# One stage more in the attention pipeline of a fused attention and mixer kernel

## The chip, the cores and the metric

The kernel runs on one core of one Trainium2 chip. The metric is device time in microseconds (us), the median of three runs. The core has five engines, each with its own queue that runs strictly in order: PE multiplies matrices (its weight loads are listed as PEld), DVE works on vectors, ACT applies functions and copies, POOL does some vector work, and SP issues most of the transfers. The engines wait for each other through semaphores.

## The reference

Three parts follow each other, on a batch of 4, a sequence of 576 and a width of 512 (8 heads of 64):

```
scores = q @ k.T / 8                       # per batch and head
scores = where(0 <= i - j < 64, scores, -1e9)
attn   = exp(scores - max(scores)); attn /= sum(attn) + 1e-9
x      = heads joined (attn @ v)           # (4, 576, 512)

mixed  = real(fft(fft(x, axis=1), axis=2))
u      = x + mixed;  un = layernorm(u)
x2     = u + relu(un @ w_ch1) @ w_ch2      # 512 -> 2048 -> 512

h      = relu(x2.T @ w_tok1) @ w_tok2      # over the tokens
u2     = x2 + h.T
out    = u2 + relu(u2 @ w_ch1') @ w_ch2'   # 512 -> 1536 -> 512
```

## The kernel before

The window of 64 keys makes attention small. It is cut into 36 units: per batch nine, of which eight hold two blocks of 64 queries for four heads each, and the ninth, the middle unit, holds the last 64 queries of all eight heads. A unit runs through seven small functions:

- `a_s` (L403): on PE, one matmul that writes the mask (L407) and sixteen in 64 x 64 tiles that add the scores (L414), into a PSUM tile `s4`. There are two such tiles, from the pool `pg`.
- `a_mx` (L421): DVE takes the row maxima (L423, tile `mx`), ACT scales them (L425, `nb`).
- `a_ex` (L428): ACT takes four exponentials from `s4` to `pb` (L433). They are the last to read `s4`.
- `a_pt` (L435): PE transposes the four pieces (L440, `pt`). `a_cp` (L442): ACT copies them back to `pb` (L443).
- `a_pv` (L445): PE multiplies with the values (L453, `o`). `a_nx` (L456): DVE divides by the sums (L460, L462, and L465, or two L470 for a middle unit) into `x`.

The loop in `front_body` (L1056) is the pipeline: in its step k it issues pieces of units k, k-1 and k-2. Into each step it also puts work of other kinds, in this order after the attention pieces:

- up to two pieces of the Fourier transform of a finished batch (`chunk`, L1071). PE runs eight matmuls in most (L531), then ACT writes the rounded half of the result and DVE the rest (`split`, L126, so L128 on ACT and L131 on DVE, tile `zt` or `zx`). In the second transform ACT copies one result (L568) and DVE reads it (L581, L582). Of the nine steps after a finished batch eight have such pieces.
- "side" work of DVE, cut by a budget in `left`: folding `x` (`fold`, tiles `pmt`, `eo`, then a split to `xh` or `xs`), splits of constants (`cs`, `dd`), statistics for the layer norm, and the conversion of the first weights (L163 to L185).

The whole front is recorded under a manual schedule, so an engine's queue holds exactly the order in which the Python code issues its work. The rest of the kernel, from about 205 us on, is a long run of matmuls (L694, L712, L729, L773), whose order a scheduler sets.

The names k, k+1 below count units; a step is one turn of the loop at L1056.

Of the kernel before, what the change touches and what calls it, by code (L numbers as in the profile page):

```python
# [29 lines left out]
def kernel(  # L30
# [351 lines left out]
    NU = len(units)  # L382
# [20 lines left out]
    def a_s(i):  # L403
        b, t, par = units[i]
        s4 = pg("s4").rearrange("p (h j) -> p h j", h=4)
        at[i, "s"] = s4
        nc.tensor.matmul(s4, lhsT=idb, rhs=cap[:, CAPS[t]:CAPS[t] + 1, :].to_broadcast([128, 4, 128]), start=True, stop=False)  # L407
        for c in range(4):
            for bl in range(2):
                if par is not None:  # L410
                    r, q0, k0 = par, 128 * (t % 2) + 64 * bl, KEY0[t][bl]
                else:
                    r, q0, k0 = bl, 0, 640
                nc.tensor.matmul(  # L414
                    s4[64 * bl:64 * bl + 64, c, :],
                    lhsT=q_t[b, t // 2][64 * r:64 * r + 64, c, q0:q0 + 64],
                    rhs=kT[b][64 * r:64 * r + 64, c, k0:k0 + 128],
                    start=False, stop=c == 3,
                )

    def a_mx(i):  # L421
        mx = sm([128, 4], F32, name="mx")
        nc.vector.tensor_reduce(out=mx, in_=at[i, "s"], axis=AX.X, op=ALU.max)  # L423
        nb = sm([128, 4], F32, name="nb")
        nc.scalar.mul(nb, mx, -scale)  # L425
        at[i, "nb"] = nb
# [18 lines left out]
    def a_pv(i):  # L445
        b, t, par = units[i]
        pb = at.pop((i, "pb"))
        o = pa("o")[:, 0:4 * (D + 1)].rearrange("p (h d) -> p h d", h=4)
        at[i, "o"] = o
        for c in range(4):  # L450
            for bl in range(2):
                rhs = v_t[b, t][:, bl, 2 * c + par, :] if par is not None else v_t[b, t][:, 0, 2 * c + bl, :]
                mm = nc.tensor.matmul(o[64 * bl:64 * bl + 64, c, :], lhsT=pb[:, 1, c, 64 * bl:64 * bl + 64], rhs=rhs)  # L453
        last_pv[0] = mm.ins

    def a_nx(i):  # L456
        b, t, par = units[i]
        o = at.pop((i, "o"))
        rs = sm([128, 4, 1], F32, name="rs")
        nc.vector.tensor_scalar_add(rs, o[:, :, D:D + 1], 1e-9)  # L460
        ri = sm([128, 4, 1], F32, name="ri")
        nc.vector.reciprocal(out=ri, in_=rs)  # L462
        x = x_tile(b, t).rearrange("p (c r d) -> p c r d", c=4, r=2)
        if par is not None:
            nc.vector.tensor_tensor(out=x[:, :, par, :], in0=o[:, :, 0:D], in1=ri.to_broadcast([128, 4, D]), op=ALU.mult)  # L465
        else:
            h0 = 64 * (b % 2)
            for r in range(2):
                a = slice(64 * r, 64 * r + 64)
                nc.vector.tensor_tensor(  # L470
                    out=x[h0:h0 + 64, :, r, :], in0=o[a, :, 0:D], in1=ri[a].to_broadcast([64, 4, D]), op=ALU.mult
                )
# [460 lines left out]
    if True:  # L933
# [91 lines left out]
        def front_body():  # L1025
            load_const()
            load_k(0, (0, 192))
            load_q(0, 0)
            load_k(0, (192, 576))
            load_v(0, 0)  # L1030
            load_k(0, (576, KW))
            load_v(0, 1)
            load_q(0, 1)
            load_q(0, 2)
            for s in range(2, 5):
                load_v(0, s)
            later = [load_cs(0), load_cs(1)]
            side = []
            ffts = []
            cur = []  # L1040
            evs = []
            side0 = []
            pcount = qcount = 0
            left = 0.0

            def chunk():
                while cur or ffts:
                    if not cur:
                        cur.append(fft(ffts.pop(0)))
                    e = next(cur[0], None)  # L1050
                    if e is not None:
                        return e
                    cur.pop()
                return None

            for k in range(NU + 3):  # L1056
                if k < NU:
                    a_s(k)
                if 0 <= k - 2 < NU:
                    a_pv(k - 2)  # L1060
                if 0 <= k - 1 < NU:
                    a_pt(k - 1)
                    a_cp(k - 1)
                if k < NU:
                    a_mx(k)
                if 0 <= k - 2 < NU:
                    a_nx(k - 2)
                if k < NU:
                    a_ex(k)
                left = min(left, 0.0) + CFG["dve"] - (1.5 if k < NU else 0.7)  # L1070
                for _ in range(2):  # L1071
                    e = chunk() if k >= 2 else None
                    if e:
                        left -= 0.25
                        e()
                if 0 <= k - 2 < NU:
                    b, t, par = units[k - 2]
                    if par == 1 and t in (1, 3):
                        side.append(fold(b, t // 2))
                    if t == 4:  # L1080
                        side.append(fold_m(b))
                while side and left > 0.0:
                    t = next(side[0], None)
                    if t is None:
                        side.pop(0)
                    else:
                        left -= t
                for (b, kt) in list(fst):
                    if kt == 2 and b not in fdone:
                        fdone.add(b)  # L1090
                        ffts.append(b)
                if k in (3, 5):
                    later.pop(0)()
                    left -= 1.1
                    if k == 3:
                        later.append(load_dd())
                if k == 7:
                    later.pop(0)()
                put_stores()
                if k < NU:  # L1100
                    b, j = divmod(k, 9)
                    if j == 1 and b + 1 < B:
                        load_k(b + 1, (0, KW))
                    if j == 3 and b + 1 < B:
                        load_q(b + 1, 0)
                        load_v(b + 1, 0)
                    if j == 5 and b + 1 < B:
                        load_v(b + 1, 1)
                    if j == 7 and b + 1 < B:
                        load_v(b + 1, 2)  # L1110
                        load_q(b + 1, 1)
                    if j == 0 and 0 < b:
                        load_v(b, 3)
                    if j == 1 and 0 < b:
                        load_v(b, 4)
                        load_q(b, 2)
                if k == 20:
                    side0.append(prep(0, u_d, 0, True, res[0, 0], ts=x_of(0)))
                if k == 30:
                    pre1[0] = prep(0, u_d, 1, True, res[1, 0], ts=x_of(1))  # L1120
                while side0 and left > 0.0 and (pcount < 7 or k >= 28):
                    t = next(side0[0], None)
                    pcount += 1
                    if t is None:
                        side0.pop(0)
                    else:
                        left -= t
                    if pcount > 7:
                        break
                while k >= 30 and left > 0.0 and qcount < 7:  # L1130
                    left -= next(pre1[0])
                    qcount += 1
                while k >= 8 and left > 0.0 and njob[0] < 2 * KA:
                    conv(1)
                    left -= 1.0
            while side0:
                if next(side0[0], None) is None:
                    side0.pop(0)
            n = 0
            tailing[0] = 1  # L1140
            while True:
                if n % 4 == 0:
                    next(gph)
                e = chunk()
                if e is None:
                    break
                e()
                if n % 2:
                    conv(1)
                elif n >= 4:  # L1150
                    next(pre1[0], None)
                put_stores()
                n += 1
                tailing[0] = n + 1
            tailing[0] = 0
            while not phase2[0]:
                next(gph)
# [70 lines left out]
        k = CFG["wb0"]  # L1228
# [155 lines left out]
```

## Time and profile before

| | |
|---|---|
| median of three runs | 986.06 us (985.76 to 986.57) |
| the profiled execution | 985.86 us, of which the span of the trace is 984.1 |
| busy share of the span: PE, DVE, ACT, POOL | 96%, 62%, 36%, 12% |
| matmuls | 6413 |

The busy shares are means over stages with different limits. The page's 40 slices show two of them: in the first five slices or so (some 150 us) PE's row changes between 8 and 9 and DVE's is at 7 or above in most, with a dip of PE and of its clock after that, and in the last three quarters PE stands at 9 in nearly every slice. The front is what the change touches; the rest starts when the front has handed over.

### The profile page before, as it was taken

What the parts mean: (1) busy time and instruction counts of PE and PEld (TensorE: products, weight loads), DVE (VectorE), ACT (ScalarE), POOL (GpSimd) and SP (SyncE); (2) the same over time, 40 slices, a digit from 0 to 9 for tenths busy, and PEclk for the clock granted to TensorE, in tenths of its full rate; (3) what the DMA queues carried; (4) which work ended last, traced back from release to release, by engine and by line L of the source; (5) the groups of instructions that cost most, each with busy time, mean ns of one, the idle gap of its engine ahead of it and who ended that gap; (6) DMA issues with size and microseconds to landing.
All of it is one profiled execution on the core that took longest, in us unless ns stands there. A gap on an engine that the chain in (4) does not pass through costs nothing.

```text
span 984.1 us, 16233 instructions
## 1 busy us (share of the span) xinstructions
PE 941.0 (96%) x6413; PEld 833.3 (85%) x6413; DVE 613.1 (62%) x1343; ACT 354.5 (36%) x761; POOL 120.8 (12%) x128
## 2 busy tenths in 40 slices
PE   8898988699999999999999999998999999999997
PEld 5676766587887899999999988876999999999997
DVE  3877777799999266676675324455775445445544
ACT  4655554333333213222232212323543333333332
POOL 0003031242222001112111000011310000000000
PEclk9888979799999999999999999999999999999999
DMA  9843220234443062454554216375411011101000
GB/s 329 295 132 135 102 66 23 91 113 133 125 142 105 5 189 73 146 171 155 174 174 131 71 40 206 108 232 167 128 45 44 1 44 44 44 1 44 23 22 22
DMA packets 58192, 105.61 MB, mean 107 GB/s; under 512 B 5250, under 2 KB 25796, under 8 KB 57732
## 3 DMA queue, kind: packets, MB, share of 16 engines
q1 hardware_dynamic: 57428, 104.25, 32.6%
q8 instruction: 50, 0.82, 0.4%
q10 hardware_dynamic: 688, 0.33, 0.1%
q14 instruction: 26, 0.21, 0.1%
HBM read 79.78 MB, written 24.77 MB: 106 GB/s over the span
## 4 chain that ended last, share of the span: by engine, by line
PE 63%; DVE 14%; DMA 3%; ACT 2%; issue 2%; POOL 0%; SPq 0%; DVEq 0%; ACTq 0%; POOLq 0%
PE zg L694 15%; PE acc L712 15%; PE zg L729 15%; PE acc L773 11%; PE acc L760 3%; PE zt L890 2%; DVE wm L180 2%; DVE we L166 2%; PE tpa L685 1%; PE zt L915 1%; DVE w2s L185 1%; DMA x2r<-x_d 1%; DVE w1s L185 1%; DVE hh L702 1%; DVE rw L179 1%
## 5 line engine op out<-in xcount | busy, mean ns | idle before, releaser
L694 PE MATMUL zg<-aT,w1s 128*128 128x384 f32 x1152 | 224.9, 344 | 3.9 <-DVE hh L702 2.9
L694 PEld LDWEIGHTS zg<-aT,w1s 128*128 128x128 f32 x1152 | 204.1, 191 | 20.1 <-DVE hh L702 12.8
L712 PE MATMUL acc<-w2s,hh 128*128 128x512 f32 x864 | 218.1, 394 | 0.0
L712 PEld LDWEIGHTS acc<-w2s,hh 128*128 128x128 f32 x864 | 160.8, 188 | 29.5
L729 PE MATMUL zg<-aT,wb 128*128 128x256 f32 x1296 | 165.5, 282 | 0.8 <-ACT wb L128 0.8
L729 PEld LDWEIGHTS zg<-aT,wb 128*128 128x128 f32 x1296 | 158.7, 189 | 1.9 <-ACT wb L128 1.0
L182 POOL TENSOR_TENSOR wm<-wm,we 128x512 f32<-128x512 f32 (+2 forms) x64 | 70.7, 1104 | 346.2 <-DVE wm L180 308.4
L702 DVE SCALAR_TENSOR_TENSOR hh<-zg,hh 128x384 fp32r<-128x384 f32 x96 | 53.2, 554 | 88.0 <-ACT hh L701 87.9
L701 ACT ACTIVATE hh<-zg 128x384 fp32r<-128x384 f32 x96 | 47.0, 490 | 168.8 <-PE zg L694 168.5
L773 PE MATMUL acc<-wb,hb 128*128 128x256 f32 x540 | 71.7, 281 | 0.0
L163 ACT ACTIVATE wm<-rw 128x512 f32<-128x512 uint32 (+2 forms) x66 | 41.9, 634 | 80.6 <-DVE w2s L185 38.9
L736 ACT ACTIVATE h<-zg 128x512 f32<-128x512 f32 x54 | 32.3, 599 | 97.1 <-PE zg L729 90.6
L773 PEld LDWEIGHTS acc<-wb,hb 128*128 128x128 f32 x540 | 67.2, 189 | 0.0
L747 DVE TENSOR_TENSOR s4h<-h 128x128 f32<-128x128 f32 x90 | 23.1, 298 | 58.8 <-ACT h L736 58.6
L773 PE MATMUL acc<-wb,ha 128*128 128x256 f32 x405 | 56.3, 281 | 0.0
L773 PEld LDWEIGHTS acc<-wb,ha 128*128 128x128 f32 x405 | 51.7, 189 | 0.2
L131 DVE TENSOR_TENSOR hb<-s4h,hb 128x512 fp32r<-128x512 f32 x45 | 31.4, 698 | 27.8 <-ACT hb L128 27.8
L180 DVE SCALAR_TENSOR_TENSOR wm<-rw,wm 128x512 f32<-128x512 int32 (+2 forms) x66 | 43.4, 658 | 5.2
L166 DVE SCALAR_TENSOR_TENSOR we<-rw,we 128x512 uint16<-128x512 uint16 (+2 forms) x66 | 43.5, 660 | 2.1
L440 PE MATMUL pt<-ident,pb 128*128 128x128 f32 x144 | 32.9, 327 | 11.8 <-ACT pb L433 11.6
L414 PEld LDWEIGHTS s<-kT,qT 64*64 64x64 f32 x576 | 33.9, 143 | 10.9 <-issue 10.9
L414 PE MATMUL s<-kT,qT 64*64 64x128 f32 x576 | 43.0, 293 | 0.0
(151 smaller groups left out, 1214.1 us busy)
## 6 DMA issues: line engine op xcount, KB each, us to landing
rw<-in_moe_w_ch_dram SPq DMA_DIRECT2D x56, 512.0 KB, 3.7
vt<-in_vx_dram SPq DMA_DIRECT2D x16, 520.0 KB, 5.4
ur<-u_d SPq DMA_DIRECT2D x28, 256.0 KB, 3.6
wb_d<-wm SPq DMA_DIRECT2D x24, 256.0 KB, 2.9
rf<-wb_d SPq DMA_DIRECT2D x24, 256.0 KB, 3.3
kT<-in_kt_dram SPq DMA_DIRECT2D x3, 1536.0 KB, 10.5
qT<-in_qt_dram SPq DMA_DIRECT2D x8, 512.0 KB, 4.7
x_d<-o SPq DMA_DIRECT2D x16, 256.0 KB, 3.5
```

The costliest lines, as they stand in the source:

```text
L163: held("a", nc.scalar.activation(out=m, in_=low, func=AF.Copy, scale=2.0 ** -52, bias=1.0))
L166: nc.vector.scalar_tensor_tensor(out=e, in0=top, scalar=0x8000, in1=e, op0=ALU.bitwise_and, op1=ALU.bitwise_or)
L180: nc.vector.scalar_tensor_tensor(out=m, in0=high, scalar=2.0 ** -20, in1=m, op0=ALU.mult, op1=ALU.add)
L182: eng.tensor_tensor(out=m, in0=m, in1=e.bitcast(BF16), op=ALU.mult)
L414: nc.tensor.matmul(s4[64 * bl:64 * bl + 64, c, :], lhsT=q_t[b, t // 2][64 * r:64 * r + 64, c, q0:q0 + 64], rhs=kT[b][64 * r:64 * r + 64, c ...
L440: nc.tensor.transpose(pt[:, c, :], pb[:, 0, c, :], ident)
L694: nc.tensor.matmul(zp, lhsT=W[f, 0][:, a, d, :], rhs=res["aT"][:, c, d, :], start=n == 0, stop=n == 11)
L701: nc.scalar.activation(out=h[:, 0], in_=zp, func=AF.Relu)
L702: nc.vector.scalar_tensor_tensor(out=h[:, 1], in0=zp, scalar=0.0, in1=h[:, 0].bitcast(F32), op0=ALU.max, op1=ALU.subtract)
L712: nc.tensor.matmul(res["acc"][c], lhsT=h[:, a, 128 * c:128 * c + 128], rhs=W[f, 1][:, w, :], start=f == 0 and i == 0, stop=f == NF - 1 and ...
L729: nc.tensor.matmul(zp[:, j], lhsT=WB[2 * p + j, 0][:, a, d, :], rhs=res["aT"][:, c, d, :], start=n == 0, stop=n == 11)
L773: nc.tensor.matmul(res["acc"][k][:, 256 * half:256 * half + 256], lhsT=t[:, a, e, :], rhs=c[i][w], start=p == 1 and n == 0 and i in (0, 4) ...
```

## The change

The loop's pieces are put into another order, and the scores and maxima of a unit are issued one step earlier than its exponentials. Those of unit 0 are issued ahead of all.

```
             for k in range(NU + 3):
+                if k == 0:
+                    a_s(0)
+                    a_mx(0)
                 if k < NU:
-                    a_s(k)
-                if 0 <= k - 2 < NU:
-                    a_pv(k - 2)
+                    a_ex(k)
                 if 0 <= k - 1 < NU:
                     a_pt(k - 1)
                     a_cp(k - 1)
-                if k < NU:
-                    a_mx(k)
                 if 0 <= k - 2 < NU:
+                    a_pv(k - 2)
                     a_nx(k - 2)
-                if k < NU:
-                    a_ex(k)
+                if k + 1 < NU:
+                    a_s(k + 1)
+                    a_mx(k + 1)
                 left = min(left, 0.0) + CFG["dve"] - (1.5 if k < NU else 0.7)
```

Pools and their buffers, the budget for the side work and everything behind the loop are as they were.

In the queue of ACT, two steps at the beginning of the first Fourier transform (`s_692` and `s_748` are the score tiles of units 12 and 13, `zt<-zp` is the rounded half of a transform piece) stood like this before:

```order
L443 COPY pb<-pt 128x512
L425 ACTIVATE nb<-mx 128x4
L433 ACTIVATE pb<-s_692,nb 128x128 x4
L128 CAST zt<-zp 128x320
L443 COPY pb<-pt 128x512
L425 ACTIVATE nb<-mx 128x4
L433 ACTIVATE pb<-s_748,nb 128x128 x4
L128 CAST zt<-zp 128x320
```

The same two steps of ACT's queue after the change, where `s_676` and `s_731` are the score tiles of units 12 and 13:

```order
L433 ACTIVATE pb<-s_676,nb 128x128 x4
L443 COPY pb<-pt 128x512
L425 ACTIVATE nb<-mx 128x4
L128 CAST zt<-zp 128x320
L433 ACTIVATE pb<-s_731,nb 128x128 x4
L443 COPY pb<-pt 128x512
L425 ACTIVATE nb<-mx 128x4
L128 CAST zt<-zp 128x320
```

Four exponentials stood between the scaled maxima and `zt` before; now `zt` follows the scaled maxima (of unit 13 in the first step) directly, and the exponentials of unit 13 come behind it.

In DVE's queue the same two steps stood like this before (`w1s`, `we` are side work):

```order
L423 TENSOR_REDUCE mx<-s_692 128x4
L460 TENSOR_SCALAR rs<-o 128x4
L462 RECIPROCAL ri<-rs 128x4
L465 TENSOR_TENSOR x<-o,ri 128x4x64
L131 TENSOR_TENSOR zt<-zp,zt 128x320
L185 TENSOR_TENSOR w1s<-wm,w1s 128x512
L423 TENSOR_REDUCE mx<-s_748 128x4
L460 TENSOR_SCALAR rs<-o 128x4
```

After the change they stand like this:

```order
L460 TENSOR_SCALAR rs<-o 128x4
L462 RECIPROCAL ri<-rs 128x4
L465 TENSOR_TENSOR x<-o,ri 128x4x64
L423 TENSOR_REDUCE mx<-s_731 128x4
L131 TENSOR_TENSOR zt<-zp,zt 128x320
L185 TENSOR_TENSOR w1s<-wm,w1s 128x512
L460 TENSOR_SCALAR rs<-o 128x4
L462 RECIPROCAL ri<-rs 128x4
```

The maxima have moved behind the three operations of `a_nx`, and they are those of the next unit. On PE a step was mask and scores, values, transposes, transform piece; now it is transposes, values, mask and scores of the next unit, transform piece.

## Rows read from the trace of the kernel before

**Rows 1.** Busy time by stage: stretch, its length, then each engine's busy time (instructions), PE's clock.

```profile
24.00:165.00 141.00, 127.19 (x1354) 97.97 (x1354) 105.62 (x265) 80.08 (x237) 21.23 (x24) 0.89 0.38 128
165.00:205.00 40.00, 27.76 (x152) 23.95 (x152) 33.33 (x72) 15.51 (x30) 13.28 (x14) 0.79 0.26 83
205.00:984.00 779.00, 764.21 (x4700) 698.59 (x4699) 466.99 (x990) 249.13 (x469) 86.09 (x86) 0.99 0.31 98
```

**Rows 2.** Waits of DVE, 24 to 165 us: us in total, times, longest us.

```profile
DVE zt L131 <- ACT zt L128: 13.3, 12, 2.0
DVE t L581 <- ACT t L568: 5.1, 6, 1.0
DVE xh L131 <- ACT xh L128: 4.2, 5, 1.2
DVE xs L131 <- ACT xs L128: 3.0, 3, 1.2
DVE zx L131 <- ACT zx L128: 2.9, 3, 1.0
DVE dd_lo L131 <- ACT dd_hi L128: 1.5, 1, 1.5
```

**Rows 3.** Timeline of DVE and ACT, one step: start, length, instruction, idle before.

```profile
109.34 0.68 DVE L423 TENSOR_REDUCE mx<-s 128x4 f32<-128x512 f32 x1
...
110.05 0.20 ACT L425 ACTIVATE nb<-mx 128x4 f32<-128x4 f32 x1 [1.67 <-DVE mx L423]
...
110.29 1.14 ACT L433 ACTIVATE pb<-s,nb 128x128 f32<-128x128 f32 x4
110.34 0.42 DVE L465 TENSOR_TENSOR xp<-o,ri 128x256 f32<-128x256 f32 x1
...
111.31 0.44 ACT L128 CAST zt<-zp 128x320 fp32r<-128x320 f32 x1
...
111.78 0.49 DVE L131 TENSOR_TENSOR zt<-zp,zt 128x320 fp32r<-128x320 f32 x1 [1.02 <-ACT zt L128]
```

**Rows 4.** Timeline of DVE, the division of one unit and what follows it.

```profile
37.54 0.15 DVE L460 TENSOR_SCALAR rs<-o 128x4 f32<-128x4 f32 x1
...
38.28 0.42 DVE L164 TENSOR_SCALAR we<-rw 128x512 uint16<-128x512 uint16 x1
```

**Rows 5.** Timeline of DVE, the step of a middle unit.

```profile
86.33 0.68 DVE L423 TENSOR_REDUCE mx<-s 128x4 f32<-128x512 f32 x1
...
87.32 0.86 DVE L470 TENSOR_TENSOR xm<-o,ri 64x256 f32<-64x256 f32 x2
88.69 0.42 DVE L581 TENSOR_TENSOR t<-ap,t 64x257 f32<-64x257 f32 x1 [0.51 <-ACT t L568]
```

**Rows 6.** Timeline of ACT, the first split of constants.

```profile
21.00 0.99 ACT L128 CAST cs_hi<-r_cs 128x960 fp32r<-128x960 f32 x1 [0.31 <-DMA r_cs<-in_c_cs_dram]
```

**Rows 7.** Timeline of DVE, the last step with maxima.

```profile
162.66 0.66 DVE L423 TENSOR_REDUCE mx<-s 128x4 f32<-128x512 f32 x1
...
165.03 0.43 DVE L581 TENSOR_TENSOR t<-ap,t 128x257 f32<-128x257 f32 x1 [0.97 <-ACT t L568]
```

**Rows 8.** Timeline of DVE, the longest wait for a transform piece.

```profile
147.15 0.49 DVE L131 TENSOR_TENSOR zt<-zp,zt 128x320 fp32r<-128x320 f32 x1 [2.02 <-ACT zt L128]
```

**Rows 9.** Timeline of PE, the mask matmuls that open two steps, at 2.4 GHz.

```profile
105.14 0.39 PE L407 MATMUL s<-cap,idb 128*128 128x512 bf16 x1
...
108.80 0.39 PE L407 MATMUL s<-cap,idb 128*128 128x512 bf16 x1
```

**Rows 10.** The same on either side of a step at 1.2 GHz.

```profile
47.80 0.63 PE L407 MATMUL s<-cap,idb 128*128 128x512 bf16 x1
...
54.38 0.46 PE L407 MATMUL s<-cap,idb 128*128 128x512 bf16 x1
```

**Rows 11.** Waits of PE and of its weight loads, 24 to 165 us.

```profile
PE pt L440 <- ACT pb L433: 11.6, 13, 1.6
...
PEld s L414 <- issue: 8.9, 30, 0.6
```

## The prediction

> **What bounds the kernel now.** I read the busy time by stage first [rows 1]. From 205 us to the end PE is busy 764.2 of 779.0 us: that part is PE's, and the change does not touch it. It starts when the front has handed over, so what the front gains the end gains. In the front, from 24 to 165 us, PE is busy 127.2 of 141.0 us but with a mean clock of 0.89, and DVE 105.6 of 141.0; neither is full. From 165 to 205 us DVE has 33.3 of 40.0, and it still finishes what the front left.
>
> Next I read the waits of DVE [rows 2]. Almost its whole idle time is waiting for ACT: 13.3 us for `zt`, 5.1 for `t`, 4.2 for `xh`, 3.0, 2.9 and 1.5 for three others, 30.0 of its 35.4 us of idle time (141.0 - 105.6). One step of the timeline tells why [rows 3]. The maxima start at 109.34, ACT scales them at 110.05, takes the exponentials at 110.29, and only behind those, at 111.31, writes the rounded half of `zt`, for which DVE's half waits until 111.78, with 1.02 us of idle time. From the maxima to that point it is 2.44 us, and `zt` has nothing to do with the exponentials: it stands behind them in ACT's queue. After it DVE does its side work and goes on to the next maxima, whose row shows no wait [rows 3]. So a step is a loop DVE - ACT - DVE plus side work, and PE is ahead of it: its transposes wait 11.6 us in all for exponentials [rows 11], and a step with a transform piece takes PE 3.66 us [rows 9], where the 16 steps from the maxima at 86.33 to those at 162.66 take 4.77 us each [rows 5, 7].
>
> **The change part by part.** No instruction is added or taken away; what counts is the order.
>
> *Exponentials behind the eviction (ACT), division ahead of the maxima (DVE).* A division takes DVE 0.74 us, from 37.54 to 38.28 [rows 4]. It used to run inside the 2.44 us; now it stands ahead of the maxima and is paid openly. Behind the maxima come now: maxima to `nb` 0.71 (109.34 to 110.05), `nb` to the next ACT instruction 0.24 (110.05 to 110.29), `zt` on ACT to `zt` on DVE 0.47 (111.31 to 111.78) [rows 3]. That is 1.42, with the division 2.16, in place of 2.44: 0.28 us less a step. The exponentials, 1.02 us from 110.29 to 111.31, and the copy behind them now run on ACT while DVE does the half of `zt`, the side work and the next division; ACT is busy 80.1 of 141.0 us [rows 1], so there is room. If a step has little side work that cover is thin, and this goes into the range.
>
> The saving holds wherever DVE waits for an ACT instruction that stood behind the exponentials: 12 times `zt`, 3 `zx`, 4 of the 6 `t`, 1 of the 5 `xh`, 2 of the 3 `xs`, and `dd_lo` [rows 2], 23 in all. The other `xh` and `xs` (but for one `xh` of a middle unit) wait for an ACT instruction that itself waits for DVE's fold just before; they stay. 23 x 0.28 = 6.4 us less.
>
> *Middle units.* There the division has two multiplications of 0.86 us together in place of one of 0.42 [rows 3, 5], so it takes 1.18 in place of 0.74. It was hidden, and from maxima to `t` it was 2.36 us, with a wait of 0.51 only [rows 5]. Now it is paid, and behind the maxima 1.35 follow (the 1.42 less the 0.07 by which a usual way to `t`, 2.37 [rows 7], is shorter than the 2.44 to `zt`): 2.53, 0.17 more, three times (two `t`, one `xh`). 0.5 us more.
>
> *The last step.* Its maxima at 162.66 and `t` at 165.03 are 2.37 us apart [rows 7]. They are now issued a step earlier. What is left there is the division, 0.74, and the copy for `t`, which stands behind exponentials that start earlier than this step. 1.6 us less. The maxima that are early by one step are paid at the beginning, where ACT waits for a transfer of constants until 21.00 anyway [rows 6], and that does not come sooner: up to about 24 us I count nothing, either way.
>
> *A piece that was late.* At 147.15 DVE waited 2.02 us, twice the usual [rows 8]. I take it, without a row for it, that PE was late there, as it would be in a stretch at 1.2 GHz. In the new order the exponentials of a unit come about a step earlier, seen from DVE, so PE may start earlier too. Between 0 and 1.0 us less (2.02 - 1.02); I take 0.5.
>
> *What PE gives back.* PE's transform piece now stands behind the scores of the next unit, and the ACT half of `zt` comes behind the maxima of these same scores. Where PE runs without a lead, `zt` waits for the piece. Its cost lies between 0 (PE is ahead as its waits show) and the whole 6.4 (each saving eaten by the piece). I take 0.9, near the first, since PE's step of 3.66 is 1.1 below DVE's of 4.77, and PE idles 13.8 us in the stretch. This term also holds the few places where ACT's side work (a fold's half, a normalization) now delays exponentials.
>
> The sum: -6.4 + 0.5 - 1.6 - 0.5 + 0.9 = -7.1 us. From the profiled execution's 985.86 us this gives 978.8 us; that execution lies 0.2 us below the median, 986.06, and I leave the prediction at 978.8.
>
> **The rivals.**
>
> *PE becomes the bound of the front.* The savings of 0.28 a step turn into waits of ACT's `zt` for PE's piece. For it: the piece is last in PE's step, and PE loses time in the new order. Scores follow the mask after a gap, 0.30 us each (8.9 us for 30) [rows 11], where the instructions go from 128 x 128 to 64 x 64 of the array. Such changes were three in a step (mask to scores, scores to values, values to transposes) and are four (transposes to values, values to mask, mask to scores, scores to piece); 35 steps x 0.30 would be 10.5 us more on PE, which idles 13.8. Against: 3.66 + 0.30 is still below 4.77. Left of the sum are the last step and the late piece against the middle units: -1.6 - 0.5 + 0.5 = -1.6, so 984.3 us.
>
> The Trainium skill, TensorEngine Tiling (Array Packing), Tiling Modes, states the rule behind this case: a change of tiling mode drains PE. The gap of 0.30 us in this trace [rows 11] agrees; what a change from 128 x 64 to 128 x 128 costs, no row here shows.
>
> *Slower: the clock.* A step with a transform piece takes PE 6.58 us at 1.2 GHz, 47.80 to 54.38 [rows 10], in place of 3.66. DVE's step would be about 4.5 (4.77 less 0.28), so each such step costs 2.1 us. The mean clock of 0.89 [rows 1] says that the front has such stretches already. If the new places of PE's idle time bring it to the lower level for more steps, the gain is gone from 7.1 / 2.1, four steps more; five or six (5.5) would cost 11.5 and give 990.3 us. Against: the front gets denser, and PE's idle share smaller. The Trainium skill, TensorE: Matmul & The Clock Gate, Part 1, says that the array falls back to its lower clock after idle time; by it fewer idle stretches speak against this case.
>
> *More than forecast.* PE is never late (0.9 back), the late piece goes wholly (0.5), the middle units cost nothing because other waits there shrink (0.5), and one stretch at 1.2 GHz does not come, worth two waits such as that at 147.15 (2.0): -11.0, so 974.9 us.
>
> **How the numbers follow.** The forecast has 0.62, with its own range of 976.5 to 981.5. PE as the bound has 0.13, the clock 0.08, more than forecast 0.17. A measurement of this kernel can tell 0.2%, 2.0 us, from no change. The forecast and the third case are faster, and of PE as the bound 0.05, since part of the savings may survive: 0.84. No change has 0.08, slower 0.08. The range goes from the third case to a little above the first rival, 975.0 to 985.0; the slower case is left out, and the ends of the others: under 0.2.
>
> **What would show it.** Right: DVE's waits for `zt` fall from 1.02 to about 0.74 us each, `t` in the last step hardly waits, the last maxima start at about 155 us, and the matmuls of the last stage take as long as before, some 764 us. ACT's waits for maxima stay its largest. Wrong: ACT's `zt` waits for PE's `zp` for more than some 2 us in all (the second case), PE's clock from 24 to 160 us is below 0.89 (the slower case), or the front ends early and the matmuls behind it start no earlier.

## The result and the profile after

The changed kernel takes 978.23 us (median of 4 runs, 976.81 to 979.15) against 985.91 us of the kernel before in the same session (985.21 to 986.57): a ratio of 0.9916, with the interval 0.9899 to 0.9934, so the gain is small but clear of the noise. The prediction was 978.8, with a range of 975.0 to 985.0. The profiled execution has a span of 976.3 us, 7.8 less than before.

Where the time comes from is seen in the busy time by stage (columns as in [rows 1]); the stretches are cut at the corresponding places:

```profile
24.00:155.00 131.00, 121.13 (x1322) 93.12 (x1321) 103.34 (x258) 73.07 (x228) 21.21 (x24) 0.92 0.41 138
...
195.00:976.00 781.00, 766.07 (x4711) 700.02 (x4709) 468.31 (x992) 249.63 (x470) 86.86 (x87) 1.00 0.31 98
```

The last stage is as long as before, 781 us in place of 779, with 766.1 us of PE in place of 764.2 [rows 1]. The gain lies in the front. The waits of DVE there, 24 to 155 us, against [rows 2]:

```profile
DVE zt L131 <- ACT zt L128: 10.0, 12, 2.2
DVE t L581 <- ACT t L568: 3.3, 6, 0.7
DVE xh L131 <- ACT xh L128: 3.0, 4, 0.8
DVE xs L131 <- ACT xs L128: 2.2, 3, 0.8
DVE zx L131 <- ACT zx L128: 1.7, 3, 0.6
DVE mx L423 <- PE s L414: 1.7, 3, 0.8
DVE dd_lo L131 <- ACT dd_hi L128: 1.0, 1, 1.0
```

Each sum of waits on ACT is smaller than before, though the longest single wait for `zt` is not (2.2 in place of 2.0), and a new one has come: three waits of the maxima for PE. One step in the timeline of DVE and ACT shows the new order, to be held against [rows 3]:

```profile
103.33 0.68 DVE L423 TENSOR_REDUCE mx<-s 128x4 f32<-128x512 f32 x1
...
104.04 0.20 ACT L425 ACTIVATE nb<-mx 128x4 f32<-128x4 f32 x1 [2.19 <-DVE mx L423]
104.15 0.41 ACT L128 CAST zt<-zp 128x320 fp32r<-128x320 f32 x1
104.46 1.14 ACT L433 ACTIVATE pb<-s,nb 128x128 f32<-128x128 f32 x4
104.59 0.49 DVE L131 TENSOR_TENSOR zt<-zp,zt 128x320 fp32r<-128x320 f32 x1 [0.58 <-ACT zt L128]
```

The rounded half `zt` now follows `nb` directly, and the exponentials run while DVE is already at its half. From the maxima to `zt` it is 1.26 us in place of 2.44, but the division now stands ahead of the maxima.

### The profile page after: what moved, and what is told of

Same layout as the page of the kernel before. It is cut to its first block, busy times and chain, and to the rows that moved or that the text cites. A ratio compares the mean times of both kernels' runs of the same rounds, so it can differ in the third digit from the quotient of the medians.

```text
span 976.3 us, 16237 instructions
## 1 busy us (share of the span) xinstructions
PE 938.4 (96%) x6413; PEld 831.2 (85%) x6413; DVE 613.9 (63%) x1343; ACT 349.6 (36%) x761; POOL 120.6 (12%) x128
## 4 chain that ended last, share of the span: by engine, by line
PE 64%; DVE 14%; DMA 3%; issue 2%; ACT 1%; POOL 0%; DVEq 0%; SPq 0%; ACTq 0%; POOLq 0%
PE zg L694 15%; PE acc L712 15%; PE zg L729 15%; PE acc L773 11%; PE acc L760 3%; DVE wm L180 2%; PE zt L890 2%; DVE we L166 2%; PE tpa L685 1%; PE zt L915 1%; DVE w2s L185 1%; DMA x2r<-x_d 1%; DVE w1s L185 1%; DVE rw L179 1%; DVE hh L702 1%
## 5 line engine op out<-in xcount | busy, mean ns | idle before, releaser
L128 ACT CAST hb<-s4h 128x512 fp32r<-128x512 f32 x45 | 27.9, 621 | 39.8 <-PE acc L773 32.3
L433 ACT ACTIVATE pb<-s,nb 128x128 f32<-128x128 f32 x144 | 40.9, 369 | 0.2
```

The lines of the kernel that those rows point to most:

```text
L433: nc.scalar.activation(out=pb[:, 0, c], in_=s4[:, c], func=AF.Exp, bias=nb[:, c:c + 1], scale=scale)
```

## The experiments

Diffs are against the changed kernel where nothing else is said. Ratios are against the kernel before, timed beside each.

**x2: the order alone.** The kernel before, with the exponentials moved behind the two pieces of the transform and nothing else; there is no extra stage.

```
                 if 0 <= k - 2 < NU:
                     a_nx(k - 2)
-                if k < NU:
-                    a_ex(k)
...
                         e()
+                if k < NU:
+                    a_ex(k)
```

> The kernel before with one edit: the exponentials of unit k are issued behind the two transform pieces of step k. No extra stage; maxima ahead of the division as before. Theory: DVE's wait for zt vanishes, since the division (0.74 us) now fills the 1.27 us from the maxima to DVE's half of zt, of which the maxima take 0.60; a step saves up to 1.1 us where DVE was the bound, and PE's step of 3.66 us is then the next limit (4.32 us a step before): 970 to 975 us. Rival (the extra stage is needed, because without it the transposes wait for late exponentials and PE stalls): 983 us or more, and PE's waits for the exponentials above the 11.6 us of before.

970.73 us (969.09 to 972.55), ratio 0.985, 0.9822 to 0.9878: faster than the change itself. One step in DVE's timeline, with the division still behind the maxima:

```profile
99.90 0.69 DVE L423 TENSOR_REDUCE mx<-s 128x4 f32<-128x512 f32 x1
100.50 0.15 DVE L460 TENSOR_SCALAR rs<-o 128x4 f32<-128x4 f32 x1
...
101.31 0.49 DVE L131 TENSOR_TENSOR zt<-zp,zt 128x320 fp32r<-128x320 f32 x1
```

In this step it is 1.41 us from the maxima to `zt`, without a wait: the division covers the way over ACT. So the exponentials behind the transform piece gain 15 us by themselves, twice what the whole change gains, and that needs no extra stage.

**x3: maxima ahead of the division.** The changed kernel with the division behind the maxima.

```
                     a_pv(k - 2)
-                    a_nx(k - 2)
                 if k + 1 < NU:
                     a_s(k + 1)
                     a_mx(k + 1)
+                if 0 <= k - 2 < NU:
+                    a_nx(k - 2)
```

> The changed kernel with the division (a_nx) issued behind the maxima of unit k+1 in place of ahead of them; on PE nothing moves. Theory: the 0.58 us of DVE's wait for zt is filled by the division; if DVE alone bounds the front, 23 x 0.58 = 13 us less than the changed kernel; with PE's step of 3.77 us as the next limit 3 to 8 us less: 970 to 975 us. Rival (PE already bounds the changed kernel's front, its waits for zt are only where the idle time shows): no change, 978 us, and ACT's zt waits for PE.

968.12 us (967.44 to 970.09), ratio 0.9826, 0.9803 to 0.9849: 10 us below the change, a little more than expected. Two rows of a step, and the front's busy time from 24 to 150 us:

```profile
91.49 0.66 DVE L423 TENSOR_REDUCE mx<-s 128x4 f32<-128x512 f32 x1
...
92.95 0.49 DVE L131 TENSOR_TENSOR zt<-zp,zt 128x320 fp32r<-128x320 f32 x1
```

```profile
24.00:150.00 126.00, 120.51 (x1386) 93.86 (x1387) 108.71 (x275) 75.97 (x232) 23.84 (x28) 0.97 0.44 146
```

From the maxima over the division to `zt` it is 1.46 us, where the change takes 0.74 for the division and 1.26 for the rest. Of 126 us PE now works 120.5, at a mean clock of 0.97: here PE is nearly the bound, which would explain that of 0.54 us a step not all becomes time (23 of them would be 12.4). x2 and x3 overlap in their intervals; with the division behind the maxima I can't tell the extra stage from none.

**x8: division ahead, no extra stage.** x2 with the division ahead of the maxima, the fourth corner of the square. The diff is against x2.

```
+                if 0 <= k - 2 < NU:
+                    a_nx(k - 2)
                 if k < NU:
                     a_mx(k)
-                if 0 <= k - 2 < NU:
-                    a_nx(k - 2)
```

> The kernel before with the exponentials moved behind the two chunk pieces of the copy of the transposed tile, as in x2_order_alone, and with the division a_nx moved ahead of the maxima; no extra stage. Theory: the place of the division is worth about 8 to 10 us (after 978.2 against 968.1 in x3, both with the extra stage), and the extra stage by itself some 3 us (x3 968.1 against x2 970.7): 977 to 982 us. Rival: the division's place matters only where the extra stage makes the scores early, since without it the maxima wait for the scores anyway while the division runs: 969 to 973 us, the time of x2.

986.64 us (984.81 to 988.84), ratio 1.0009, 0.9992 to 1.0025: no gain at all over the kernel before. Both expectations failed, the theory by nearly 5 us. The four corners (the kernel before lay between 985.5 and 985.9 us beside each):

| | division ahead of the maxima | behind them |
|---|---|---|
| no extra stage, exponentials behind the piece | 986.6 (x8) | 970.7 (x2) |
| extra stage | 978.2 (the change) | 968.1 (x3) |

So the division's place is worth 16 us without the stage and 10 with it, and the stage 8.4 us where the division is ahead. Waits of DVE in x8, 24 to 165 us, since its front is as long as that of the kernel before:

```profile
DVE xh L131 <- ACT xh L128: 8.0, 7, 2.0
DVE xs L131 <- ACT xs L128: 5.0, 3, 1.9
...
DVE dd_lo L131 <- ACT dd_hi L128: 2.2, 1, 2.2
```

What I had left out is the side work of DVE. Its ACT halves (`xh`, `xs`, `dd`) still stand behind the exponentials of the step, and the division, which used to cover 0.74 us of that wait, is gone from there: the longest for `xh` grows from 1.2 us [rows 2] to 2.0. In the change the extra stage puts these halves ahead of the next exponentials. The same `xh` in x8, and then in the change:

```profile
49.67 1.15 ACT L433 ACTIVATE pb<-s,nb 128x128 f32<-128x128 f32 x4
...
51.35 0.69 DVE L131 TENSOR_TENSOR xh<-eo,xh 128x514 fp32r<-128x514 f32 x1 [1.96 <-ACT xh L128]
```

```profile
45.40 0.60 ACT L128 CAST xh<-eo 128x514 fp32r<-128x514 f32 x1
45.91 1.13 ACT L433 ACTIVATE pb<-s,nb 128x128 f32<-128x128 f32 x4
46.04 0.69 DVE L131 TENSOR_TENSOR xh<-eo,xh 128x514 fp32r<-128x514 f32 x1 [0.78 <-ACT xh L128]
```

The waits for the three are 15.2 us in x8 and 6.2 in the change. The same instructions can be laid side by side in the two traces: at the last `t` the change leads x8 by 11.2 us (156.68 against 167.89). Of this lead 9.0 us grow at the side halves (`cs`, `dd`, `xh`, `xs`) and 2.1 at the last step; what PE costs either kernel in its stretches at 1.2 GHz nearly cancels. The medians are only 8.4 us apart, since the profiled execution of x8 is the slowest of its ten (988.84 us). This account is read from the traces and was not tried by itself.

**x4: PE's clock kept up.** In the changed kernel PE idles 3.14 us up to 87.45, for the exponentials of unit 20. They stand behind ACT's half of `xh`, which itself waits 2.50 us for DVE's fold. Timeline of the change around it:

```profile
86.51 0.62 ACT L128 CAST xh<-eo 128x514 fp32r<-128x514 f32 x1 [2.50 <-DVE eo L487]
87.04 1.13 ACT L433 ACTIVATE pb<-s,nb 128x128 f32<-128x128 f32 x4
87.45 1.25 PE L440 MATMUL pt<-ident,pb 128*128 128x128 f32 x4 [3.14 <-ACT pb L433]
...
94.74 0.43 ACT L128 CAST zt<-zp 128x320 fp32r<-128x320 f32 x1 [1.49 <-PE zp L531]
95.20 0.49 DVE L131 TENSOR_TENSOR zt<-zp,zt 128x320 fp32r<-128x320 f32 x1 [2.19 <-ACT zt L128]
```

Behind the idle time PE's granted clock is 0.50, that is 1.2 GHz:

```profile
88.00:92.00 4.00, 4.00 (x36) 2.95 (x35) 3.18 (x11) 2.60 (x9) 0.00 (x0) 0.50 0.85 332
92.00:96.00 4.00, 4.00 (x26) 3.42 (x24) 1.79 (x4) 1.95 (x8) 0.00 (x0) 0.50 0.95 376
```

x4 lets PE write the mask 13 times more into the score tile in that gap; the write that opens the sum of the scores comes behind them.

```
         at[i, "s"] = s4
+        for _ in range(13 if i == 21 else 0):
+            nc.tensor.matmul(s4, lhsT=idb, rhs=cap[:, CAPS[t]:CAPS[t] + 1, :].to_broadcast([128, 4, 128]), start=True, stop=True)
```

> The changed kernel with 13 more mask matmuls ahead of the scores of unit 21 (their result is overwritten), in the 3.1 us in which PE waits from 84.3 to 87.4 us for the exponentials of unit 20. Theory (the low clock from 88 to 97.5 us makes the transform pieces late and costs the waits of 2.19, 0.52 and 1.13 us in place of 0.58, 0 and 0.58): the clock stays at 1.00 in that stretch and the time falls by 2 to 3 us, to about 976 us. Rival (the pieces are late for another reason, or the loss is made up later): no change, 978 us.

975.55 us (973.4 to 980.92), ratio 0.9906, 0.987 to 0.9942. The times of x4 and of the change can't be told apart by their intervals. Run by run they part with the clock: the change has 0.975 to 0.979 as its mean in all four runs, three runs of x4 have 0.984 to 0.988 and take 973.4 to 975.61 us, less than any of the change, and the fourth, of 980.92 us, has 0.973. In the profiled execution of x4 the clock stays at the upper level, and the same `zt` waits are the usual ones.

```profile
88.00:92.00 4.00, 3.85 (x44) 2.84 (x43) 3.19 (x11) 2.61 (x9) 0.00 (x0) 1.00 1.00 339
92.00:96.00 4.00, 4.00 (x49) 3.36 (x48) 3.28 (x9) 2.87 (x10) 0.00 (x0) 1.00 0.98 391
```

```profile
93.83 0.49 DVE L131 TENSOR_TENSOR zt<-zp,zt 128x320 fp32r<-128x320 f32 x1 [0.58 <-ACT zt L128]
...
105.68 0.49 DVE L131 TENSOR_TENSOR zt<-zp,zt 128x320 fp32r<-128x320 f32 x1 [0.59 <-ACT zt L128]
```

The `zt` that starts at 105.68 here starts at 108.21 in the change, 2.5 us later. Ahead of the gap x4 lay 0.3 us behind the change, so this one stretch costs the front some 2.9 us. x3 does not fall to the lower clock there either (1.00 from 84 to 96 us): its lead over the change grows from 3.5 us at the `xs` (87.39 against 90.87) to 7.4 two `zt` later (92.95 against 100.36). So some 4 of the 10 us by which x3 is faster come at this place, and the price of the division's place holds the clock as well.

**x5: one change of array mode less.** x3 with the values (and the division) behind the scores, so that PE's step is transposes, mask, scores, values, piece. The diff is against the changed kernel.

```
+                if k + 1 < NU:
+                    a_s(k + 1)
+                    a_mx(k + 1)
                 if 0 <= k - 2 < NU:
                     a_pv(k - 2)
                     a_nx(k - 2)
-                if k + 1 < NU:
-                    a_s(k + 1)
-                    a_mx(k + 1)
```

> As the kernel with the maxima ahead of the division, and on PE the scores of unit k+1 also ahead of the values of unit k-2, so that a step has three changes of array part (mask to scores, scores to values, values to transform piece) in place of four. Theory (the fourth change cost the 0.11 us by which PE's step grew from 3.66 to 3.77 us, and with the maxima ahead PE is now nearly the bound): PE's step is 3.66 us again and the time falls by 1 to 3 us against the 968.1 us of that kernel: 965 to 967 us. Rival (PE is not the bound there): 968 us, no change.

965.26 us (962.31 to 973.63), ratio 0.9795, 0.9745 to 0.9845, which overlaps with x3. The step is measured without doubt, though: mask matmuls of PE in the change, and then in x5, all at 2.4 GHz.

```profile
100.85 0.39 PE L407 MATMUL s<-cap,idb 128*128 128x512 bf16 x1
104.62 0.39 PE L407 MATMUL s<-cap,idb 128*128 128x512 bf16 x1
```

```profile
95.39 0.38 PE L407 MATMUL s<-cap,idb 128*128 128x512 bf16 x1
99.06 0.38 PE L407 MATMUL s<-cap,idb 128*128 128x512 bf16 x1
```

3.77 us in the change with four changes of mode; 3.67 in x5 with three, as 3.66 before [rows 9]. Whether the shorter step gains time stays open. In the profiled executions the front of x5 hands over no earlier than that of x3 (the last `t` starts at 146.32 in x5, at 145.51 in x3): x5 fell to 1.2 GHz twice (0.52 from 84 to 88 us, 0.50 from 126 to 130). The 2.6 us by which its span is shorter come behind the front.

**x1: exponentials later still.** The changed kernel with the exponentials of unit k at the end of the step, behind the maxima of unit k+1.

```
-                if k < NU:
-                    a_ex(k)
...
                     a_s(k + 1)
                     a_mx(k + 1)
+                if k < NU:
+                    a_ex(k)
```

> The extra stage is kept (scores and maxima of unit k+1 in step k, division ahead of the maxima), but the exponentials of unit k are issued behind the maxima of unit k+1, so they stand ahead of the transform's eviction in ACT's queue, as they did before the change. Theory (the gain comes from taking the exponentials out of DVE's wait for the eviction): from maxima to DVE's half of zt it is 2.44 us again, and the division of 0.74 us now adds to it, 23 steps x 0.74 = 17 us above the kernel before: about 1000 us. Rival (the earlier scores and maxima are what helps, wherever the exponentials stand): as the changed kernel, about 978 us.

1038.53 us (1033.29 to 1040.91), ratio 1.053, 1.049 to 1.057: slower, as expected, but by far more than expected. From 24 to 84 us PE's clock is 0.50 throughout, and the timeline shows each engine waiting for the next:

```profile
24.00:84.00 60.00, 48.34 (x374) 34.51 (x374) 30.32 (x72) 22.59 (x66) 2.32 (x2) 0.50 0.43 141
```

```profile
41.07 1.12 ACT L433 ACTIVATE pb<-s,nb 128x128 f32<-128x128 f32 x4
41.47 1.25 PE L440 MATMUL pt<-ident,pb 128*128 128x128 f32 x4 [1.29 <-ACT pb L433]
...
46.27 0.69 DVE L423 TENSOR_REDUCE mx<-s 128x4 f32<-128x512 f32 x1 [1.27 <-PE s L414]
47.00 0.20 ACT L425 ACTIVATE nb<-mx 128x4 f32<-128x4 f32 x1 [3.44 <-DVE mx L423]
47.11 1.12 ACT L433 ACTIVATE pb<-s,nb 128x128 f32<-128x128 f32 x4
```

Exponentials, transposes, scores, maxima, exponentials: one serial ring of 6.0 us, since the exponentials stand in ACT's queue behind the `nb` of the next unit. With the exponentials so late the extra stage ties the engines together.

**x6: the scores at the head of the step.** x1 with scores first, then values, transposes, maxima and exponentials, to take the transposes out of that ring. The diff is against the kernel before.

```
-                if k < NU:
-                    a_s(k)
+                if k == 0:
+                    a_s(0)
+                    a_mx(0)
+                if k + 1 < NU:
+                    a_s(k + 1)
                 if 0 <= k - 2 < NU:
                     a_pv(k - 2)
+                    a_nx(k - 2)
                 if 0 <= k - 1 < NU:
                     a_pt(k - 1)
                     a_cp(k - 1)
-                if k < NU:
-                    a_mx(k)
-                if 0 <= k - 2 < NU:
-                    a_nx(k - 2)
+                if k + 1 < NU:
+                    a_mx(k + 1)
                 if k < NU:
                     a_ex(k)
```

> Again the extra stage with the exponentials ahead of the transform's eviction in ACT's queue, but now PE keeps the order of the kernel before (scores, values, transposes, transform piece, with the scores of unit k+1), so that scores no longer stand behind transposes that wait for late exponentials. The first such kernel took 1038.5 us where 1000 was expected, with PE at 1.2 GHz from 20 to 80 us. Theory (its excess came from that loop over PE, and what is left is the division paid ahead of a wait of 2.3 us): 985.5 + 23 x 0.74 = about 1002 us, between 996 and 1006. Rival (the extra stage with exponentials ahead costs the excess by itself): 1030 us or more.

1041.06 us (1038.69 to 1041.96), ratio 1.0543, 1.0513 to 1.0574. That expectation fell: no better than x1. PE waits for ACT at another place, 24 to 150 us:

```profile
PE s L407 <- ACT pb L433: 31.7, 17, 4.0
```

There are two score tiles, and the mask of unit k+1 needs the one that the exponentials of unit k-1 read last; these come at the very end of the step before. So the ring closes over the tile instead of the queue. Together x1 and x6 say that, with two score tiles and in the orders tried, scores that are early need exponentials that are early as well, as the change has them.

**x7: x5 with PE kept busy at the end of the front.** 50 matmuls into a tile that is overwritten, ahead of the last batch's first transform piece. The diff is against x5.

```
             zp = pz("zp")[:, 0:KN]
+            for _ in range(50 if last and (eo, m) == (0, 0) else 0):
+                nc.tensor.matmul(zp[:, 0:256], lhsT=idb, rhs=cap[:, 0:2, :], start=True, stop=True)
```

> As x5, with 50 more mask matmuls (their result is overwritten) ahead of the first transform piece of the last batch, where PE has almost nothing to do for some 9 us while DVE folds, and then runs a transform piece, transposes and a block of zg at 1.2 GHz. Theory (that low clock is on the path to the last stage): zg's first block takes about 2 us in place of 4.6, and the time falls by 2 to 4 us against x5. Rival (DVE's conversion of weights is the bound behind it and takes the gain back): the same time as x5.

962.84 us (960.06 to 972.33), ratio 0.9774, 0.972 to 0.9828. It has the lowest median of all, but its interval overlaps with that of x5. The clock fell all the same a little later, as the two rows of x7 show:

```profile
150.00:158.00 8.00, 5.15 (x40) 4.14 (x38) 6.06 (x15) 1.87 (x4) 2.18 (x3) 0.99 0.37 115
158.00:166.00 8.00, 7.53 (x28) 7.13 (x29) 5.57 (x15) 3.78 (x8) 1.54 (x1) 0.58 0.25 72
```

In the profiled executions the filler brings next to nothing. x7 leads x5 by 4.6 us already at the last `t` (141.70 against 146.32), ahead of the filler, where the two kernels are the same, and by 4.9 us in the span. The first block of `zg` takes 4.6 us in both. The lead ahead of the filler goes with the clock (from 126 to 130 us it is 1.00 in x7, 0.50 in x5), and so do the single runs: those of x5 go from 973.63 us at a mean clock of 0.97 to 962.31 at 0.99, those of x7 from 972.33 at 0.975 to 960.06 at 0.992.

## Why the prediction was right, point by point

- **What bounds the kernel.** Right. The last stage is unchanged and starts earlier, by nearly all that the front gained: the last `t` starts 8.35 us earlier (165.03 to 156.68), the span ends 7.8 earlier. One reading was too broad: 3.66 us is PE's step with a piece of the first transform. With one of the second it is 4.64 (masks at 118.79 and 123.43), and there PE is hardly ahead of DVE's mean step of 4.77.
- **The step.** The mechanism was right and the size was off. I had 0.28 us a step; the step shows 2.44 less 0.74 and 1.26, that is 0.44. The term at fault is "`nb` to the next ACT instruction 0.24": it was read between `nb` and exponentials that need `nb`. `zt` does not, and starts 0.11 us behind (104.04 to 104.15). 23 x 0.44 is 10.1 in place of 6.4. With the same instructions laid side by side in both traces, DVE's lead over the kernel before does grow by 0.40 to 0.55 us at 19 of the 23 places; the other four come below. `zt` waits 0.58 us now at most places, where I had said 0.74.
- **Middle units.** The size was right for a `t`, too large for the three. The division takes 1.29 us now and the way behind the maxima 1.22, which is 2.51 in place of 2.36, 0.15 more against the forecast 0.17. DVE's lead falls by 0.14 and 0.11 us at the two `t` and stays as it is at the `xh`: 0.3 us more in place of 0.5.

```profile
81.53 0.15 DVE L460 TENSOR_SCALAR rs<-o 128x4 f32<-128x4 f32 x1
...
82.82 0.69 DVE L423 TENSOR_REDUCE mx<-s 128x4 f32<-128x512 f32 x1
...
84.04 0.42 DVE L581 TENSOR_TENSOR t<-ap,t 64x257 f32<-64x257 f32 x1 [0.53 <-ACT t L568]
```

- **The last step.** Right. DVE's lead over the kernel before grows from 6.82 us at the last `zx` to 8.35 at `t`, 1.5 against the forecast 1.6, and `t` has no wait (the last maxima start at 152.67, where I had said about 155):

```profile
153.93 0.48 DVE L131 TENSOR_TENSOR zx<-zpx,zx 2x320 fp32r<-2x320 f32 x1 [0.58 <-ACT zx L128]
...
156.68 0.43 DVE L581 TENSOR_TENSOR t<-ap,t 128x257 f32<-128x257 f32 x1
```

- **The late piece.** The cause that I had assumed was right, the gain was not there. The kernel before runs at 0.50 of its clock from 134 to 142 us. The change dips there too, to 0.66 and 0.91 in the two halves of that time, and of the 2.02 us of waiting [rows 8] 1.13 are left. But the maxima of the same step now wait 0.78 us for PE:

```profile
139.77 0.69 DVE L423 TENSOR_REDUCE mx<-s 128x4 f32<-128x512 f32 x1 [0.78 <-PE s L414]
141.59 0.49 DVE L131 TENSOR_TENSOR zt<-zp,zt 128x320 fp32r<-128x320 f32 x1 [1.13 <-ACT zt L128]
```

  At this piece DVE's lead grows by 0.25 us, less than the 0.44 of a usual step, so nothing of the 0.5 came.
- **What PE gives back.** Undersized: 0.9 forecast. The terms as measured are -10.1 + 0.3 - 1.5 + 0.0 = -11.3. DVE's lead grows by 8.0 us, from 0.3 at 28 us, ahead of the first of the 23 places, to 8.35 at the last `t`, so 3.3 us came back. They are at four of the 23 places, all `zt`: some 2.8 us at the two in the stretch at 1.2 GHz that x4 takes away (`zt` at 95.20 and 100.36), and 0.5 at the late piece and the `zt` ahead of it. ACT's `zt` waits 2.4 us for PE in all, a little over the 2 that I had named as a sign of PE as the bound, but 1.9 of it is that one stretch. A saving undersized by 3.7 us, a loss undersized by 2.4 and a late piece that brought nothing nearly cancelled: that the total came within 0.6 us is luck in good part.
- **The rivals.** PE as the bound fell in its price: 35 more changes of mode at 0.30 us were 10.5, while a step grew by 0.11 (3.66 to 3.77), 3.9 in all. The Trainium skill, TensorEngine Tiling (Array Packing), Tiling Modes, states that a change of tiling mode drains PE; the trace agrees that it costs something, at a third of the gap that I had taken. That gap was a mean over both levels of the clock: at 2.4 GHz the wait ahead of the scores is 0.23 us. The clock as a loss did not decide: 0.92 in the front against 0.89, but its mechanism was there once. More than forecast, 974.9, wanted no such stretch: without it x4 has a median of 975.55 us, near that figure, though its time can't be told from the change's by the intervals.
- **What the prediction did not see.** The division ahead of the maxima is a loss of some 10 us inside the change (x3). It was in my sum, as 0.74 us paid openly, but only as a deduction: I never asked what the change would be worth without it. Nor did I see that the exponentials alone could be moved (x2), nor that what the stage itself brings lies, as the traces read, in the side work (x8).

## What to carry to other kernels

In a queue that runs in order, ask of each instruction that another engine waits for what stands ahead of it without being needed by it, and move that back. Then ask what the waiting engine can do in the meantime: work that stood inside a wait was free, and moved ahead of it, it is paid in full. When a change has several parts, price each by itself and each pair of them: here one part gained and another gave half of it back, and what the second cost depended on the third. And read the granted clock beside each time: single runs of one kernel here lie up to 12 us apart with it (x7).

## What the runs showed of the hardware

- An ACT instruction behind `nb` that does not need its result starts 0.11 us after it, one that needs it 0.24 us ([rows 3], and the step above).
- PE idled 3.14 us up to 87.45, and then its granted clock was 0.50 for the next eight microseconds at least; with 13 matmuls in that gap it stayed at 1.00 in the profiled execution of x4.
- One more change of array mode made a step of PE 0.11 us longer, while the gap ahead of the scores is 0.30 as a mean over both levels of the clock [rows 11].
